# Two token groups of expert 1's second half move into the attention's instruction list, their sums pass through DRAM, and the routing rows get a buffer per group

## The chip, the cores and the metric

The kernel runs on one NeuronCore of one Trainium2 chip. The metric is device time in microseconds (us), less is better. Before the change three runs took 2198.85, 2198.92 and 2199.71 us, median 2198.92. The profile is of one further execution, which took 2201.63 us; its trace spans 2199.9 us. Engines: PE (TensorE), DVE (VectorE), ACT (ScalarE), POOL (GpSimd), and SP (SyncE), whose queue issues most DMAs.

## The reference: what is computed

Three stages follow one another. First a delta-rule attention (4 batches, 8 heads, 768 steps, head size 48), whose output, 3072 tokens by 384, feeds a dense mixture of 8 experts, whose output feeds a second mixture in which each token goes to one expert.

```python
state = state + bt[:, :, :, None] * np.einsum('bhd,bhe->bhde', kt, vt - v_old)     # attention, per step
...
for _ in range(8):                                # first mixture: Sinkhorn-scaled weights P
    P /= P.sum(1, keepdims=True) + 1e-09
    P /= P.sum(0, keepdims=True) + 1e-09
    P *= N / E
for e in range(E):
    out += P[:, e:e + 1] * (np.maximum(x @ w1[e], 0.0) @ w2[e])
...
expert_idx = np.argmax(logits, axis=1)            # second mixture: one expert for each token
out[mask] = gate_w[mask, None] * (np.maximum(x[mask] @ w1[e], 0.0) @ w2[e])
```

Every matrix product is made of three half-precision products (high by high, low by high, high by low), so weights and activations are kept as a high and a low float16 part.

## The kernel before, in words

The tokens lie in 24 tiles of 128 (`NT`), or 6 groups of 512 (`NG`). The hidden size 1024 is 8 blocks of 128 (`KF`); half of it is 4 blocks (`FH`).

**The attention's list.** The attention is written as nodes with costs and dependencies, and `Sched.run` puts them into one order for each engine when the program is built. Into the same list go matmuls of the first mixture: expert 0 whole and the first half of expert 1's hidden blocks, both as units of 256 tokens (`moe_unit`). Their sums need the Sinkhorn weights, which are known only after all of the attention, so they go unscaled to DRAM: ACT copies the sum out of PSUM into the tile `yo` (one buffer), and SP stores it to `y0d` or `y1d`. For these sums the list has one PSUM buffer (`py` in the pool `ps2`). At the list's end stands a piece of expert 1's second half for group 0 of 512 tokens: the first layer (36 matmuls of 512 columns, L1065) and the second layer of the first token tile (12 matmuls of 384 columns, L1078).

**The dense stage.** After the list PE works through the rest of the first mixture in written order. `accb`, the accumulator for 24 tiles, is loaded from `y0d` by six DMAs (L1212). For expert 1 each group loads `yh` from `y1d` (L375); `mlp1` is the first layer, four hidden blocks of nine matmuls, each followed by ACT's relu (high part, L336) and DVE's `hhl` instruction (low part, L337); `mlp2` then makes four token tiles with two PSUM buffers (`py` in `ps3`). Each tile's sum is put into `accb` by ACT's scaling (L384) and two DVE instructions, one for `yh` (L385), one for `py` (L388). Experts 2 to 6 follow with all eight hidden blocks.

**The work beside it.** `run` steps a generator of one group, and after each third step gives one step to every background queue (`bg`). The queue `prepq` holds, in this order: ten empty steps, the preparation of expert 2's weights (`prep_w`: load a half into `st`, six DVE maxima `wmx` at L296, a scale, six ACT and six DVE instructions that split it into `W`; then the other half), `setup2` (a small preparation of the second mixture with a PE transpose `pen`), then the weights of the second mixture. All engines run their instructions in program order. So an instruction that waits holds up what stands behind it on its engine, and this holds for DMAs that SP issues too.

**The routing stage.** Expert 7 and the routing of the second mixture are a second list. For each group `route_group` fills the tile `row` (token number and weight, L1435) and scatters its rows into a DRAM table by four indirect DMAs of POOL (L1461). `row` and the row indices `ri` have two buffers each, so a group takes the buffers of two groups before, and the COPY of L1435 waits until that group's scatter has landed.

Of the kernel before, what the change touches and what calls it, by code (L numbers as in the profile page):

```python
# [165 lines left out]
def kernel(  # L166
# [78 lines left out]
    ones32 = res.tile([128, 128], F32, name="ones32")  # L245
    nc.gpsimd.memset(ones32, 1.0)
    pe = {}
    pye = []
    nc.scalar.activation(out=ivg[0:1], in_=ones32[0:1, 0:1], func=AF.Sqrt)

    def step(gen, n=1):
# [87 lines left out]
    def mlp1(W, XH, XL, n, HH, HL, fs=0):  # L339
        per = 512 // n  # L340
        for f0 in range(fs, KF, per):
            pt = ps1.tile([128, 512], F32, name="pt")
            for j in range(per):
                f = f0 + j
                po = pt[:, j * n:j * n + n]
                i = 0
                for kk in range(KD):
                    for lhsT, rhs in (
                        (w1v(W, 0, kk, f), XH[:, kk, :]),
                        (w1v(W, 0, kk, f), XL[:, kk, :]),  # L350
                        (w1v(W, 1, kk, f), XH[:, kk, :]),
                    ):
                        nc.tensor.matmul(out=po, lhsT=lhsT, rhs=rhs, start=(i == 0), stop=(i == 3 * KD - 1))  # L353
                        i += 1
                    if f == f0 + per - 1 and kk == KD - 1:
                        relu_split(pt, HH[(f0 - fs) // per], HL[(f0 - fs) // per])
                    yield 1

    def mlp2(W, HH, HL, fs=0):
        py = ypool[0].tile([128, 512], F32, name="py")  # L360
        n = 0
        for f in range(fs, KF):
            for lhsT, rhs in ((HH(f - fs), w2v(W, 0, f)), (HH(f - fs), w2v(W, 1, f)), (HL(f - fs), w2v(W, 0, f))):
                nc.tensor.matmul(out=py[:, 0:DM], lhsT=lhsT, rhs=rhs, start=(n == 0), stop=(n == 3 * (KF - fs) - 1))  # L364
                n += 1
            if f < KF - 1:
                yield None
        yield py

    def moe1_group(e, W, g):  # L370

        fs, x = (FH, "b") if e == 1 else (0, e)
        if e == 1:
            yh_ = st2.tile([128, 4, DM], F32, name="yh", tag="yh", bufs=2)
            nc.sync.dma_start(out=yh_, in_=y1d[4 * g:4 * g + 4].rearrange("t p d -> p t d"))  # L375
        if (e, g) != (1, 0):
            yield from mlp1(W, xh[g], xl[g], 512, hh, hl, fs)
        for j in range(4):
            t = 4 * g + j
            sl = slice(128 * j, 128 * j + 128)  # L380
            for py in pye[:1] if (e, t) == (1, 0) else mlp2(W, lambda f: hh[f][:, sl], lambda f: hl[f][:, sl], fs):
                if py is not None:
                    if e == 1:
                        nc.scalar.activation(out=acc[t], in_=acc[t], func=AF.Copy, scale=pe[0][:, t:t + 1])  # L384
                        nc.vector.scalar_tensor_tensor(  # L385
                            out=acc[t], in0=yh_[:, j], scalar=pe[1][:, t:t + 1], in1=acc[t], op0=ALU.mult, op1=ALU.add
                        )
# [31 lines left out]
    with (  # L419
# [446 lines left out]
        def Q(name, eng, cost, fn, deps=(), prio=0.0, **kw):  # L866
            NN[name] = nd(eng, cost, fn, flat(NN[d] for d in deps if d in NN), prio=prio, name=f"{name[0]}.{name[1]}", **kw)
# [111 lines left out]
        def f():  # L979
            nc.sync.dma_start(out=c16, in_=cst16)  # L980
            nc.sync.dma_start(out=cs, in_=cst)
# [75 lines left out]
        o1 = {}
        pn = None
        for f_ in range(FH):
            for kk in range(KD):  # L1060
                def f(slot=None, f_=f_, kk=kk):
                    if kk == 0:
                        o1[f_] = ps1.tile([128, 512], F32, name="pt")
                    for x, (wv, xv) in enumerate(((0, xh), (0, xl), (1, xh))):
                        nc.tensor.matmul(out=o1[f_], lhsT=w1v(W1, wv, kk, FH + f_), rhs=xv[0][:, kk], start=kk == 0 and x == 0, stop=kk == KD - 1 and x == 2)  # L1065
                Q((f"h{f_}_{kk}", "e1"), "P", 648, f, [pn] if pn else [("xb", 0), mend] + w1a, 2e6,
                  ps=("pt", 1) if kk == 0 else None, cols=1536, moe=True)
                pn = (f"h{f_}_{kk}", "e1")
            wr = [mend]
            Q((f"rl{f_}", "e1"), "A", 478, lambda f_=f_: nc.scalar.activation(out=hh[f_], in_=o1[f_], func=AF.Relu), [pn] + wr, NT - 1.0)  # L1070
            Q((f"rs{f_}", "e1"), "V", 602, lambda f_=f_: nc.vector.scalar_tensor_tensor(
                out=hl[f_], in0=o1[f_], scalar=0.0, in1=hh[f_], op0=ALU.max, op1=ALU.subtract), [(f"rl{f_}", "e1")], NT - 1.0, frees=(f"h{f_}_0", "e1"))
        for f_ in range(FH):
            def f(slot=None, f_=f_):
                if f_ == 0:
                    pye.append(ps2.tile([128, 512], F32, name="py"))
                for x, (a_, b_) in enumerate(((hh, 0), (hh, 1), (hl, 0))):
                    nc.tensor.matmul(out=pye[0][:, 0:DM], lhsT=a_[f_][:, 0:128], rhs=w2v(W1, b_, FH + f_),  # L1078
                                     start=(f_ == 0 and x == 0), stop=(f_ == FH - 1 and x == 2))
            Q((f"g{f_}", "e1"), "P", 488, f, [pn, (f"rs{f_}", "e1")] + w1, 2e6, ps=("py", 1) if f_ == 0 else None, cols=1152, moe=True)  # L1080
            pn = (f"g{f_}", "e1")
# [124 lines left out]
    queue(prepq, iter([1] * 10))
    queue(prepq, prep1(2))
    queue(prepq, setup2())
    for e in range(E):
# [3 lines left out]
    for e in range(1, E - 1):  # L1213
        W = Ws[e % 2]
        assert e in wready, e
        if e > 1:
            mk_pe(e)
            prepq.insert(min(1, len(prepq)), prep1(e + 1))
            queue(prepq)
        for g in range(NG):  # L1220
            run(moe1_group(e, W, g))
    while bgs:
        bg()

# [88 lines left out]
    def route_tile(g, j):  # L1313
# [14 lines left out]
        node2(("sn", id_), "A", 520, f, [("acc", t), ("sc", g - 2)], prio=pr)  # L1328

        def f():  # L1330
            o["mx"] = sm.tile([128, 2], F32, name="xmx")
# [54 lines left out]
    def route_group(g):  # L1386
# [19 lines left out]
        lgs = [("lg", 4 * g + j) for j in range(T)]  # L1406
        sns = [("sn", 4 * g + j) for j in range(T)]

        q("m", lambda: vt.tensor_reduce(out=tl("m", [T]), in_=R()[0], op=ALU.max, axis=AX.X), lgs + [("sc", g - 2)], cost=100)
# [6 lines left out]
        q("s1", lambda: vt.tensor_scalar(out=R()[1], in0=R()[1], scalar1=1e-36, scalar2=None, op0=ALU.max), sns + [("sc", g - 2)])  # L1416
# [315 lines left out]
```

## Time and profile before

| what | before |
|---|---|
| runs, us | 2198.85, 2198.92, 2199.71 |
| profiled execution, us | 2201.63 |
| its span, us | 2199.9 |
| PE busy | 2055.6 (93%) |
| DVE busy | 1237.0 (56%) |
| ACT busy | 850.0 (39%) |
| POOL busy | 282.1 (13%) |

Span and busy times are of the profiled execution, with busy time as a share of the span. A row of the trace says when an instruction (or several alike, x12) began, how long it took, and in brackets how long its engine had been idle before it and what ended that. The trace's times count from the span's start; expert 1's dense part runs from 709.7 to 806.1 us, the routing stage from about 1745 to 1985 us.

### The profile page before, as it was taken

The page shows a single profiled execution, that of the slowest core. Times are in us where ns is not written, and L with a number is a line of the kernel's source. Part 1 is how long each engine was busy: PE and PEld are TensorE (multiplying, and loading weights), DVE is VectorE, ACT ScalarE, POOL GpSimd, SP SyncE. Part 2 cuts the span into 40 slices and gives each one's busy share as a digit, 9 for nine tenths or more (in the row PEclk, how much of TensorE's full clock was granted, in tenths as well). Part 3 has the DMA queues.
Part 4 walks back from the last instruction along what each step waited for, and adds up shares of the span by engine and source line. Part 5 has one row for each costly group of instructions (what it writes and reads, how often), then busy time and mean ns, then how long its engine had stood idle before and what let it go on. Part 6 is the DMA issues. An engine that isn't in the chain of part 4 may idle for free. (4 is left out here: it accounts for less than half of the span.)

```text
span 2199.9 us, 46260 instructions
## 1 busy us (share of the span) xinstructions
PE 2055.6 (93%) x19352; PEld 1298.4 (59%) x19352; DVE 1237.0 (56%) x2820; ACT 850.0 (39%) x1594; POOL 282.1 (13%) x324
## 2 busy tenths in 40 slices
PE   3689999989989899999999999999999989999999
PEld 2577777767765445555555555555555545557777
DVE  7988788888763564555545455554553245552111
ACT  6666656566532232232223222322221134352332
POOL 5333223122200000000000000000000000112221
PEclk7589999999999999999999999999999999999999
DMA  4557666566533230222131222213120001049765
GB/s 105 96 105 125 114 110 116 103 117 117 123 110 109 94 105 29 87 84 89 58 115 62 83 87 86 87 58 115 58 87 1 1 19 26 19 126 355 270 237 203
DMA packets 436615, 224.92 MB, mean 102 GB/s; under 512 B 377565, under 2 KB 419329, under 8 KB 430003
## 3 DMA queue, kind: packets, MB, share of 16 engines
q1 hardware_dynamic: 432114, 211.67, 35.9%
q0 software_dynamic: 4288, 10.25, 1.3%
q8 instruction: 154, 2.52, 0.5%
q14 instruction: 59, 0.48, 0.1%
HBM read 138.28 MB, written 50.36 MB: 86 GB/s over the span
## 5 line engine op out<-in xcount | busy, mean ns | idle before, releaser
L353 PE MATMUL pt<-big,W 128*128 128x512 f16 x2340 | 512.8, 379 | 3.5 <-DVE hhl L337 2.0
L353 PEld LDWEIGHTS <-W 128*128 128x128 f16 x2340 | 229.0, 98 | 277.7 <-issue 7.0
L364 PE MATMUL py<-W,hhl 128*128 128x384 f16 x1716 | 302.0, 327 | 8.9 <-DVE accb L388 8.9
L336 ACT ACTIVATE hhl<-pt 128x512 f16<-128x512 f32 x140 | 83.5, 596 | 520.2 <-PE pt L353 514.6
L364 PE MATMUL py<-W,ttb 128*128 128x384 f16 x1440 | 253.6, 326 | 0.0
L364 PEld LDWEIGHTS <-hhl 128*128 128x128 f16 x1716 | 168.4, 98 | 125.3 <-issue 11.6
L388 DVE SCALAR_TENSOR_TENSOR accb<-py,pet,accb 128x384 f32<-128x384 f32 x144 | 88.8, 617 | 197.3 <-PE py L364 195.3
L364 PEld LDWEIGHTS <-ttb 128*128 128x128 f16 x1440 | 140.9, 98 | 93.1
L827 PE MATMUL pt<-xring,W 128*128 128x256 f16 x1296 | 185.0, 277 | 1.4 <-DVE hhl L840 1.0
L337 DVE SCALAR_TENSOR_TENSOR hhl<-pt,hhl 128x512 f16<-128x512 f32 x140 | 96.7, 691 | 149.9 <-ACT hhl L336 149.9
L851 PE MATMUL py<-W,hhl 128*128 128x384 f16 x864 | 174.7, 332 | 5.0 <-ACT yo L861 3.8
L337 DVE SCALAR_TENSOR_TENSOR ttb<-pt,ttb 128x512 f16<-128x512 f32 x120 | 82.9, 690 | 92.7 <-ACT ttb L336 92.6
L296 DVE TENSOR_REDUCE wmx<-st 128x1 f32<-128x512 f32 x168 | 110.4, 677 | 41.1 <-DMA st<-in_moe_w_dram 41.1
L303 POOL PARTITION_ALL_REDUCE wma<-wm x28 | 10.4, 370 | 959.5 <-DVE wm L301 959.5
L336 ACT ACTIVATE ttb<-pt 128x512 f16<-128x512 f32 x120 | 71.5, 596 | 136.9 <-PE pt L353 136.4
L1266 PEld LDWEIGHTS <-W 128*128 128x128 f16 x1008 | 90.6, 98 | 57.1 <-issue 7.1
L827 PEld LDWEIGHTS <-W 128*128 128x128 f16 x1296 | 113.5, 100 | 16.5 <-issue 1.3
L1286 PE MATMUL py<-W,hhl 128*128 128x384 f16 x624 | 110.8, 330 | 0.0
L1266 PE MATMUL pt<-big,W 128*128 128x512 f16 x432 | 98.5, 379 | 5.4 <-DVE hhl L1272 5.4
L851 PEld LDWEIGHTS <-hhl 128*128 128x128 f16 x864 | 74.9, 99 | 44.9 <-issue 7.5
L1272 DVE SCALAR_TENSOR_TENSOR ttb<-pt,ttb 128x512 f16<-128x512 f32 x50 | 34.6, 691 | 113.2 <-ACT ttb L1271 113.1
L1272 DVE SCALAR_TENSOR_TENSOR hhl<-pt,hhl 128x512 f16<-128x512 f32 x52 | 35.8, 688 | 91.2 <-ACT hhl L1271 91.1
(368 smaller groups left out, 3163.3 us busy)
## 6 DMA issues: line engine op xcount, KB each, us to landing
st<-in_moe_w_dram SPq DMA_DIRECT2D x28, 1536.0 KB, 9.9
W<-w2d SPq DMA_DIRECT2D x18, 1536.0 KB, 8.1
w2d<-big SPq DMA_DIRECT2D x16, 1536.0 KB, 6.2
big<-w2d SPq DMA_DIRECT2D x8, 1536.0 KB, 7.7
accb<-w2d SPq DMA_DIRECT2D x8, 1536.0 KB, 9.1
big<-kqc SPq DMA_DIRECT2D x90, 128.0 KB, 3.7
big<-KQ SPq DMA_DIRECT2D x84, 96.0 KB, 3.4
st<-PTc SPq DMA_DIRECT2D x42, 128.0 KB, 3.2
```

Source lines behind the costliest of these rows:

```text
L296: nc.vector.tensor_reduce(out=mx[:, c:c + 1], in_=st[:, c * CW:c * CW + CW], op=ALU.max, axis=AX.X, apply_absolute_value=True)
L303: nc.gpsimd.partition_all_reduce(ma, m1, channels=128, reduce_op=bass.bass_isa.ReduceOp.max)
L336: nc.scalar.activation(out=oh, in_=pt, func=AF.Relu)
L337: nc.vector.scalar_tensor_tensor(out=ol, in0=pt, scalar=0.0, in1=oh, op0=ALU.max, op1=ALU.subtract)
L353: nc.tensor.matmul(out=po, lhsT=lhsT, rhs=rhs, start=(i == 0), stop=(i == 3 * KD - 1))
L364: nc.tensor.matmul(out=py[:, 0:DM], lhsT=lhsT, rhs=rhs, start=(n == 0), stop=(n == 3 * (KF - fs) - 1))
L388: nc.vector.scalar_tensor_tensor(out=acc[t], in0=py[:, 0:DM], scalar=pe[x][:, t:t + 1], in1=acc[t], op0=ALU.mult, op1=ALU.add)
L827: nc.tensor.matmul(out=o[g4][:, 256 * j:256 * j + 256], lhsT=w1v(W, wv, kk, f_), rhs=XR[:, xv, kk], start=(kk == 0 and x == 0), stop=(kk = ...
L851: nc.tensor.matmul(out=o["py"][:, 0:DM], lhsT=a_[f_ // per][:, c_:c_ + 128], rhs=w2v(W, b_, f_), start=(f_ == 0 and x == 0), stop=(f_ == n ...
L1266: nc.tensor.matmul(out=po, lhsT=w1v(W, wv, kk, f), rhs=xv[:, kk, :], start=(kk == 0 and x == 0), stop=(kk == KD - 1 and x == 2))
L1272: V((f"rs{q_}", id_), lambda q_=q_: nc.vector.scalar_tensor_tensor(out=HL[q_], in0=o[q_], scalar=0.0, in1=HH[q_], op0=ALU.max, op1=ALU.sub ...
L1286: nc.tensor.matmul(out=o["py"][:, 0:DM], lhsT=a_[f // per][:, c_:c_ + 128], rhs=w2v(W, b_, f), start=(f == 0 and x == 0), stop=(f == KF - ...
```

## The change

Groups 0 and 1 (`GW = 2`) of expert 1's second half are computed wholly in the attention's list: two first layers and eight second-layer tiles. Their sums are not put into `accb` there; ACT copies each one to `yo` and SP stores it, unscaled, to a new DRAM array `y2d`. In the dense stage expert 1 begins with group 2. The sums of groups 0 and 1 are put into `accb` by a second background queue (`woven_group`), which loads `yg` from `y1d` and `yz` from `y2d` for a tile, scales and adds. The background queues get a step after each second step of expert 1's groups and no longer each third, the ten empty steps are gone, and `yh` is loaded in halves. In the routing `row` and `ri` get one buffer for each group, and the waits on a scatter two groups before become waits on the instructions that last read the other tiles.

```diff
+GW = 2
+    y2d = DR.tile([4 * GW, 128, DM], F32, name="y2d")
...
-        if e == 1:
-            yh_ = st2.tile([128, 4, DM], F32, name="yh", tag="yh", bufs=2)
-            nc.sync.dma_start(out=yh_, in_=y1d[4 * g:4 * g + 4].rearrange("t p d -> p t d"))
+        for j in range(0, 4 if e == 1 else 0, 2):
+            yh_.append(st2.tile([128, 2, DM], F32, name="yh", bufs=2))
+            nc.sync.dma_start(out=yh_[-1], in_=y1d[4 * g + j:4 * g + j + 2].rearrange("t p d -> p t d"))
...
+    def first_acc(t, yh_):
+        nc.scalar.activation(out=acc[t], in_=acc[t], func=AF.Copy, scale=pe[0][:, t:t + 1])
+        nc.vector.scalar_tensor_tensor(out=acc[t], in0=yh_, scalar=pe[1][:, t:t + 1], in1=acc[t], op0=ALU.mult, op1=ALU.add)
+
+    def woven_group(g):
+        for t in range(4 * g, 4 * g + 4):
+            yg = st2.tile([128, DM], F32, name="yg", bufs=2)
+            nc.sync.dma_start(out=yg, in_=y1d[t])
+            yz = st2.tile([128, DM], F32, name="yz", bufs=2)
+            nc.sync.dma_start(out=yz, in_=y2d[t])
+            yield 1
+            yield 1
+            yield 1
+            first_acc(t, yg)
+            nc.vector.scalar_tensor_tensor(
+                out=acc[t], in0=yz, scalar=pe["b"][:, t:t + 1], in1=acc[t], op0=ALU.mult, op1=ALU.add
+            )
+            yield 1
...
+        for g in range(GW):
...
+                def f(t_=t_, g=g, o1=o1):
+                    ob = hp.tile([128, DM], F32, name="yo")
+                    nc.scalar.copy(out=ob, in_=o1["py"][:, 0:DM])
+                    nc.sync.dma_start(out=y2d[4 * g + t_], in_=ob)
+                Q((f"yo{t_}", e1), "A", 413, f, [pn], NT - 1.0, frees=(f"g{t_}_0", e1))
...
-    queue(prepq, iter([1] * 10))
...
-        for g in range(NG):
-            run(moe1_group(e, W, g))
+        if e == 1:
+            queue([], iter([1] * 4), *(woven_group(g) for g in range(GW)))
+        for g in range(GW if e == 1 else 0, NG):
+            run(moe1_group(e, W, g), 2 if e == 1 else 3)
...
-            o["row"] = s2.tile([128, T, 2], I32, name="row")
+            o["row"] = s2.tile([128, T, 2], I32, name="row", bufs=NG)
             vt.tensor_copy(out=o["row"][:, :, 0], in_=toki[:, 4 * g:4 * g + 4])
-        q("ro", f, [("sc", g - 2)])
+        q("ro", f, [])
...
+            o["ri"] = s2.tile([128, T], I32, name="ri", bufs=NG)
```

PE's matmuls keep their order, but for `pen`, which moves to an earlier place. Three other places move. On SP, at the list's end, stood before:

```order
L862 DMA y0d<-yo 128x384 x2
L862 DMA y1d<-yo 128x384 x4
L1212 DMA accb<-y0d 128x4x384 x6
L375 DMA yh<-y1d 128x4x384 x2
L287 DMA st<-in_moe_w_dram 128x3x1024
L375 DMA yh<-y1d 128x4x384 x2
```

and there stands now:

```order
L879 DMA y1d<-yo 128x384 x4
L1107 DMA y2d<-yo 128x384 x8
L1238 DMA accb<-y0d 128x4x384 x6
L377 DMA yh<-y1d 128x2x384 x2
L288 DMA st<-in_moe_w_dram 128x3x1024
L398 DMA yg<-y1d 128x384
L400 DMA yz<-y2d 128x384
```

The eight stores to `y2d`, each behind an ACT copy of a list tile, have come ahead of the loads of `accb`, and the weight load into `st` still follows behind `yh`.

On DVE, from the list's end on, stood before:

```order
L1071 SCALAR_TENSOR_TENSOR hhl<-pt,hhl 128x512 x4
L385 SCALAR_TENSOR_TENSOR accb<-yh,pet,accb 128x384
L388 SCALAR_TENSOR_TENSOR accb<-py,pet,accb 128x384
L385 SCALAR_TENSOR_TENSOR accb<-yh,pet,accb 128x384
L388 SCALAR_TENSOR_TENSOR accb<-py,pet,accb 128x384
L385 SCALAR_TENSOR_TENSOR accb<-yh,pet,accb 128x384
L388 SCALAR_TENSOR_TENSOR accb<-py,pet,accb 128x384
L385 SCALAR_TENSOR_TENSOR accb<-yh,pet,accb 128x384
L388 SCALAR_TENSOR_TENSOR accb<-py,pet,accb 128x384
L337 SCALAR_TENSOR_TENSOR hhl<-pt,hhl 128x512 x4
```

and there stands now:

```order
L1091 SCALAR_TENSOR_TENSOR hhl<-pt,hhl 128x512 x8
L338 SCALAR_TENSOR_TENSOR hhl<-pt,hhl 128x512 x3
L297 TENSOR_REDUCE wmx<-st 128x1
L338 SCALAR_TENSOR_TENSOR hhl<-pt,hhl 128x512
L297 TENSOR_REDUCE wmx<-st 128x1 x2
L393 SCALAR_TENSOR_TENSOR accb<-yh,pet,accb 128x384
L386 SCALAR_TENSOR_TENSOR accb<-py,pet,accb 128x384
L297 TENSOR_REDUCE wmx<-st 128x1
L393 SCALAR_TENSOR_TENSOR accb<-yg,pet,accb 128x384
L405 SCALAR_TENSOR_TENSOR accb<-yz,pet,accb 128x384
L297 TENSOR_REDUCE wmx<-st 128x1
```

The first maximum over `st` now stands ahead of the fourth `hhl` of the first dense group, where before the dense stage began with additions into `accb`.

On DVE, in the routing stage, while PE is in a group's second layer, stood before:

```order
L1456 CAST qri<-qrr 128x4
L1272 SCALAR_TENSOR_TENSOR ttb<-pt,ttb 128x512 x3
L1435 COPY row<-toki 128x4
L1272 SCALAR_TENSOR_TENSOR ttb<-pt,ttb 128x512
L1477 SCALAR_TENSOR_TENSOR accb<-py,pet,accb 128x384
```

and there stands now:

```order
L1486 CAST ri<-qrr 128x4
L1300 SCALAR_TENSOR_TENSOR ttb<-pt,ttb 128x512 x4
L1508 SCALAR_TENSOR_TENSOR accb<-py,pet,accb 128x384
L1360 TENSOR_REDUCE xmx<-accb 128x1
L1362 TENSOR_SCALAR xmx<-xmx 128x1
```

The COPY into `row` no longer stands among the `ttb` instructions; all six copies stand at the head of the routing stage.

## Rows read from the trace of the kernel before

**Rows 1.** Timeline of PE: start us, duration us, line, operation; in brackets idle, releaser.

```profile
698.05 2.11 PE L851 MATMUL py<-W,hhl 128*128 128x384 f16 x12 [0.61 <-ACT yo L861]
700.00 7.93 PE L1065 MATMUL pt<-big,W 128*128 128x512 f16 x36
707.77 2.11 PE L1078 MATMUL py<-W,hhl 128*128 128x384 f16 x12
709.72 4.06 PE L364 MATMUL py<-W,hhl 128*128 128x384 f16 x24
722.34 4.00 PE L364 MATMUL py<-W,hhl 128*128 128x384 f16 x12 [8.56 <-DVE accb L388]
...
742.02 7.93 PE L353 MATMUL pt<-big,W 128*128 128x512 f16 x36
...
806.08 9.88 PE L353 MATMUL pt<-big,W 128*128 128x512 f16 x45
817.14 0.35 PE L1157 MATMUL pen<-cs,ench 8*128 8x8 f32 x3 [1.19 <-DVE ench L1152]
```

**Rows 2.** Windows: busy us (and count) of PE, PEld, DVE, ACT, POOL; clock, DMA, GB/s.

```profile
715.00:720.00 5.00, 0.00 (x0) 0.00 (x0) 0.31 (x1) 0.00 (x0) 0.00 (x0) 0.65 1.06 373
720.00:722.30 2.30, 0.00 (x0) 0.00 (x0) 2.08 (x5) 0.00 (x0) 0.00 (x0) 0.50 1.06 414
...
709.70:806.10 96.40, 86.92 (x459) 45.30 (x457) 57.01 (x104) 30.23 (x54) 1.68 (x4) 0.95 0.36 123
806.10:839.20 33.10, 31.67 (x173) 16.72 (x172) 15.13 (x39) 7.82 (x13) 0.35 (x1) 1.00 0.08 30
```

**Rows 3.** Timeline of DVE, routing stage.

```profile
1806.59 0.17 DVE L1435 COPY row<-toki 128x4 int32<-128x4 int32 x1 [9.77 <-DMA tab<-row,qri]
```

**Rows 4.** Timeline of PE, routing stage.

```profile
1799.20 1.95 PE L1286 MATMUL py<-W,ttb 128*128 128x384 f16 x11
1807.41 0.50 PE L1286 MATMUL py<-W,ttb 128*128 128x384 f16 x1 [6.26 <-DVE ttb L1272]
...
1811.55 1.95 PE L1286 MATMUL py<-W,ttb 128*128 128x384 f16 x9
```

**Rows 5.** Timeline of PE, next group's boundary.

```profile
1847.31 0.34 PE L1286 MATMUL py<-W,ttb 128*128 128x384 f16 x1 [1.77 <-DVE ttb L1272]
```

**Rows 6.** Timeline of ACT: the last two copies of the list.

```profile
697.52 0.48 ACT L861 COPY yo<-py 128x384 f32<-128x384 f32 x1 [1.69 <-PE py L851]
700.24 0.48 ACT L861 COPY yo<-py 128x384 f32<-128x384 f32 x1 [2.24 <-PE py L851]
```

**Rows 7.** The list's stores of yo (whole span to 720): from issue to landing, us.

```profile
DMA to landing us min/median/max: 1.8/1.8/4.4
```

**Rows 8.** Timeline of the DMAs that SP issues.

```profile
701.25 5.47 SPq L1212 DMA_DIRECT2D accb<-y0d  x6
706.77 4.96 SPq L375 DMA_DIRECT2D yh<-y1d  x2
```

**Rows 9.** The page's DMA issues: KB of one, median us to landing.

```profile
st<-in_moe_w_dram SPq DMA_DIRECT2D x28, 1536.0 KB, 9.9
```

**Rows 10.** Timeline of DVE, dense stage of expert 1 and after.

```profile
719.69 0.62 DVE L385 SCALAR_TENSOR_TENSOR accb<-yh,pet,accb 128x384 f32<-128x384 f32 x1 [10.40 <-DMA yh<-y1d]
...
752.41 0.61 DVE L385 SCALAR_TENSOR_TENSOR accb<-yh,pet,accb 128x384 f32<-128x384 f32 x1
753.14 0.62 DVE L388 SCALAR_TENSOR_TENSOR accb<-py,pet,accb 128x384 f32<-128x384 f32 x1
753.67 0.68 DVE L296 TENSOR_REDUCE wmx<-st 128x1 f32<-128x512 f32 x1
...
762.59 0.75 DVE L276 SCALAR_TENSOR_TENSOR W<-st,w0s,W 128x512 f16<-128x512 f32 x1 [0.73 <-ACT W L275]
...
815.77 0.15 DVE L1109 RECIPROCAL nrc<-nsr 8x1 f32<-8x1 f32 x1 [2.29 <-ACT nsr L1107]
```

**Rows 11.** The second half's load into st, 760 to 800 us.

```profile
DMA to landing us min/median/max: 7.0/7.0/7.0
```

More of the change, by code (lines that the diff above doesn't have):

```diff
@@ L247 @@
     pe = {}
-    pye = []
     nc.scalar.activation(out=ivg[0:1], in_=ones32[0:1, 0:1], func=AF.Sqrt)
@@ L372, in moe1_group @@
         fs, x = (FH, "b") if e == 1 else (0, e)
-        if e == 1:
-            yh_ = st2.tile([128, 4, DM], F32, name="yh", tag="yh", bufs=2)
-            nc.sync.dma_start(out=yh_, in_=y1d[4 * g:4 * g + 4].rearrange("t p d -> p t d"))
-        if (e, g) != (1, 0):
-            yield from mlp1(W, xh[g], xl[g], 512, hh, hl, fs)
+        yh_ = []
+        for j in range(0, 4 if e == 1 else 0, 2):
+            yh_.append(st2.tile([128, 2, DM], F32, name="yh", bufs=2))
+            nc.sync.dma_start(out=yh_[-1], in_=y1d[4 * g + j:4 * g + j + 2].rearrange("t p d -> p t d"))
+        yield from mlp1(W, xh[g], xl[g], 512, hh, hl, fs)
         for j in range(4):
@@ L380, in moe1_group @@
             sl = slice(128 * j, 128 * j + 128)
-            for py in pye[:1] if (e, t) == (1, 0) else mlp2(W, lambda f: hh[f][:, sl], lambda f: hl[f][:, sl], fs):
+            for py in mlp2(W, lambda f: hh[f][:, sl], lambda f: hl[f][:, sl], fs):
                 if py is not None:
                     if e == 1:
[L384 to L387, printed above, removed]
+                        first_acc(t, yh_[j // 2][:, j % 2])
                     nc.vector.scalar_tensor_tensor(
@@ L1055 @@
             Q(("xb", g), "D", 1300, f, bigdeps(g) + [("x1", 4 * g + 1), ("x1", 4 * g + 3)], NT + 1.0 + g, lat=1500.0)
[L1057 to L1081, printed above, removed]
+        pn = mend
@@ new lines, with f @@
+        for g in range(GW):
+            e1 = f"e1{g}"
+            o1 = {}
+            wr = pn
+            for f_ in range(FH):
+                for kk in range(KD):
+                    def f(slot=None, f_=f_, kk=kk, g=g, o1=o1):
+                        if kk == 0:
+                            o1[f_] = ps1.tile([128, 512], F32, name="pt")
+                        for x, (wv, xv) in enumerate(((0, xh), (0, xl), (1, xh))):
+                            nc.tensor.matmul(out=o1[f_], lhsT=w1v(W1, wv, kk, FH + f_), rhs=xv[g][:, kk], start=kk == 0 and x == 0, stop=kk == KD - 1 and x == 2)
+                    Q((f"h{f_}_{kk}", e1), "P", 648, f, [pn] if f_ or kk else [pn, ("xb", g)] + w1a, 2e6 + g,
+                      ps=("pt", 1) if kk == 0 else None, cols=1536, moe=True)
+                    pn = (f"h{f_}_{kk}", e1)
+                Q((f"rl{f_}", e1), "A", 478, lambda f_=f_, o1=o1: nc.scalar.activation(out=hh[f_], in_=o1[f_], func=AF.Relu), [pn, wr], NT - 1.0)
+                Q((f"rs{f_}", e1), "V", 602, lambda f_=f_, o1=o1: nc.vector.scalar_tensor_tensor(
+                    out=hl[f_], in0=o1[f_], scalar=0.0, in1=hh[f_], op0=ALU.max, op1=ALU.subtract), [(f"rl{f_}", e1)], NT - 1.0, frees=(f"h{f_}_0", e1))
+            for t_ in range(4):
+                for f_ in range(FH):
+                    def f(slot=None, f_=f_, t_=t_, o1=o1):
+                        if f_ == 0:
+                            o1["py"] = ps2.tile([128, 512], F32, name="py")
+                        for x, (a_, b_) in enumerate(((hh, 0), (hh, 1), (hl, 0))):
+                            nc.tensor.matmul(out=o1["py"][:, 0:DM], lhsT=a_[f_][:, 128 * t_:128 * t_ + 128], rhs=w2v(W1, b_, FH + f_),
+                                             start=(f_ == 0 and x == 0), stop=(f_ == FH - 1 and x == 2))
+                    Q((f"g{t_}_{f_}", e1), "P", 488, f, [pn, (f"rs{f_}", e1)] + w1, 2e6 + g, ps=("py", 1) if f_ == 0 else None, cols=1152, moe=True)
+                    pn = (f"g{t_}_{f_}", e1)
+                def f(t_=t_, g=g, o1=o1):
[3 more added lines that the diff above has]
+                Q((f"yo{t_}", e1), "A", 413, f, [pn], NT - 1.0, frees=(f"g{t_}_0", e1))
@@ L1327, in f @@
             nc.scalar.activation(out=junk, in_=acc[t], func=AF.Square, accum_out=R()[1][:, j:j + 1])
-        node2(("sn", id_), "A", 520, f, [("acc", t), ("sc", g - 2)], prio=pr)
+        node2(("sn", id_), "A", 520, f, [("acc", t), ("rw", g - 2)], prio=pr)
         def f():
@@ L1407, in route_group @@
         sns = [("sn", 4 * g + j) for j in range(T)]
-        q("m", lambda: vt.tensor_reduce(out=tl("m", [T]), in_=R()[0], op=ALU.max, axis=AX.X), lgs + [("sc", g - 2)], cost=100)
+        q("m", lambda: vt.tensor_reduce(out=tl("m", [T]), in_=R()[0], op=ALU.max, axis=AX.X), lgs + [("ri", g - 2), ("rw", g - 2)], cost=100)
         q("l2", lambda: vt.tensor_tensor(out=tl("l2", [T, E]), in0=R()[0], in1=b3(o["m"]), op=ALU.subtract), ["m"], cost=100)
@@ L1414, in route_group @@
         q("oh", lambda: vt.tensor_tensor(out=tl("oh", [T, E], F16), in0=b2_(eio), in1=b3(o["fi"]), op=ALU.is_equal), ["fi"], cost=100)
-        q("s1", lambda: vt.tensor_scalar(out=R()[1], in0=R()[1], scalar1=1e-36, scalar2=None, op0=ALU.max), sns + [("sc", g - 2)])
+        q("s1", lambda: vt.tensor_scalar(out=R()[1], in0=R()[1], scalar1=1e-36, scalar2=None, op0=ALU.max), sns + [("rw", g - 2)])
         q("s0", lambda: nc.scalar.activation(out=tl("sr", [T]), in_=R()[1], func=AF.Ln), ["s1"], "A", 220)
@@ L1455, in route_group, with f @@
         q("rr", lambda: vt.tensor_reduce(out=tl("rr", [T]), in_=o["rk"], op=ALU.add, axis=AX.X), ["rm"], cost=100)
-        q("ri", lambda: vt.tensor_copy(out=tl("ri", [T], I32), in_=o["rr"]), ["rr"])
+        def f():
+            o["ri"] = s2.tile([128, T], I32, name="ri", bufs=NG)
+            vt.tensor_copy(out=o["ri"], in_=o["rr"])
+        q("ri", f, ["rr"])
         def f():
```

## The prediction, made before the changed kernel had run

> **What bounds the kernel now.** I read the busy times of the engines first: PE is busy in 93% of the span, so a change moves the time where it opens or closes a gap of PE, or lets another engine pass it. Then I read PE's timeline, bracket by bracket, in the two stretches that the change touches. At the list's end PE runs the list's last first layer and one tile (700.00 to 709.72), then two tiles of the dense stage, and then it waits 8.56 us for DVE [rows 1]. DVE's timeline names what DVE waited for: `yh`, which landed at about 719.5 [rows 10], behind the six loads of `accb` on the same queue [rows 8]. PE comes back at the lower of its two clocks, 1.2 GHz (granted share 0.50 in the window before it resumes [rows 2]): 12 matmuls take 4.00 us for 2.11 [rows 1]. In the routing stage PE waits 6.26 us and then 1.77 us for a `ttb` instruction of DVE [rows 4, 5]; DVE stood at the COPY into `row`, 9.77 us the first time, until a scatter had landed [rows 3]. Last I read the windows for how full DVE is in expert 1's dense part: 57.0 us in 96.4 [rows 2].
>
> All sums are made against the profiled execution, 2201.63 us, which is 2.7 above the median 2198.92; I put the differences on the median. PE's order is unchanged but for `pen`, so I follow PE from 700.00.
>
> **Step 1, the list gets longer.** From start to start a first layer takes 7.77 us (700.00 to 707.77) and a tile 1.95 us (707.77 to 709.72) where the next may follow at once [rows 1]. In the list there is one PSUM buffer, and each tile waits for ACT's copy of the one before: the copies of such a pair lie 2.72 us apart [rows 6], with PE idle 0.61 [rows 1]. So a group costs 7.77 + 1.95 + 3 x 2.72 = 17.9 us, two 35.8, and the dense stage begins at 735.8. `yo` has one buffer too, so a copy needs the store before it to have landed: 0.48 + 1.8 = 2.3 us, under 2.72 [rows 6, 7]; with the longest landing, 4.4, the six pairs would cost 2.2 us more each, 13 in all, my upper bound. Before, group 2 began at 742.02 [rows 1], so PE is 6.2 us ahead here: the old wait and its slow clock are gone, 3 x 2 x 0.77 = 4.6 us is paid for copies.
>
> The Trainium skill, "DMA: Bandwidth & Descriptors", section "Anatomy of one DMA — SWDGE (gpsimd) path", puts a DMA at 2.0 us plus its bytes at 436 GB/s, most of the 2.0 being the receipt of the write. By this a store of 192 KB takes 2.45 us, a copy cannot follow before 2.9 us, and step 1 would cost about 1.3 us more; the row with 1.8 decides.
>
> **Step 2, the loads start late.** SP issues in order, and the first load of `accb` stands right behind the last store: it was issued at 701.25, 1.25 us after the matmuls that follow the last stored tile began [rows 8, 1]. That was 8.5 us ahead of the dense stage. Now eight more stores stand ahead of it, the last behind a copy at the list's very end, so the first load goes out at 735.8 + 1.25 = 737.0, when dense work has already begun. Before, DVE had the first `yh` 18.4 us after that issue (719.69 less 701.25): seven transfers of 768 KB. Now these are followed by expert 2's weights, 1536 KB [rows 9], 4.2 us more at the 373 GB/s of the full queue [rows 2]. So `st` is there at 737.0 + 18.4 + 4.2 = 759.7.
>
> **Step 3, a new wait.** The ten empty steps were what kept DVE's first maximum over `st` away from this load. Now it stands ahead of the fourth `hhl` of group 2, which PE needs for the last quarter of its first tile. PE ends the first layer at 743.5 and three quarters of a tile at 745.0. DVE resumes at 759.7, runs one maximum (0.6) and the `hhl` (0.7), and PE goes on at 761.0: 16.0 us idle in place of 8.56. The slow clock afterwards costs the 1.9 us of [rows 1]. Left of expert 1 are then 0.5 + 3 x 1.95 + 3 x 15.57 = 53.1 us (a dense group is 7.77 + 4 x 1.95), so without any further wait it ends at 816.0, against 806.08 before [rows 1]: 9.9 us later.
>
> **Step 4, DVE becomes the bound.** The additions of groups 0 and 1 are still made in the dense stage, so DVE keeps its 48 additions, while PE loses two groups to the list. DVE's work before was 57.0 us; four `hhl` fewer make 54.2. To this come `setup2` and the first maxima of the next preparation, as the steps now run faster: they were 15.1 us of the next window less eight `hhl`/`ttb` (5.5) and four additions (2.5), about 7 [rows 2]. Three `hhl` come before the stall (2.1), which leaves about 59 us behind 759.7. An addition that depends on the one before starts 0.73 us after it, though one lasts 0.61 [rows 10]; over the 24 pairs that is some 2 us more: 61. And DVE waits in it, for reasons that its order fixes: the second half of the weights can be loaded only when the first has been split, lands 7.0 us after its issue [rows 11], and DVE has about 4 us of additions and `hhl` to do meanwhile (3); twice the first split waits for ACT (0.73 each [rows 10], 1.5); the root in `setup2` takes ACT 2.3 us, behind ACT's queue (3) [rows 10]; `pen` sends DVE to PE and back, with the `hhl` behind it (3); four short ones for PE (2). That is 12.5, so DVE's last addition of expert 1 ends near 759.7 + 61 + 12.5 = 833, and PE, at most two tiles ahead of it, leaves expert 1 at about 832. Late against before: 832 - 806.1 = 26. I see this on PE as waits for `hhl` in the second and third dense group (2 to 3 us each), one for `py` of about 3 us while the second weight half lands, and one of 3 to 4 at `pen`. In the next expert `pen`'s 1.2 us is saved [rows 1]: 24.8. The bounds are 9.9 (DVE hides all) and 32 (those 3 us waits also lower the clock).
>
> **Step 5, the routing rows.** Both COPYs that waited for a scatter now stand at the stage's head and wait for nothing. PE's tiles, 3.9 us each here, would have been at 1799.20 + 2 x 1.95 = 1803.1 where the row says 1811.55: 8.45 us [rows 4]. The second wait is 1.77 [rows 5]. What is late next? The last `ttb` could have followed its predecessor by 1.9 us and be done 2 us before PE's need, and no other instruction of DVE or ACT waits for a scatter. Gain 10.2; from the other side at least 0, if PE stopped for something hidden behind.
>
> The extra traffic (1.5 MB stored and loaded again) is hidden: the queue has 0.36 of its time taken in this stretch [rows 2]. The eight loads from `y1d` replace two of equal bytes.
>
> **Sum.** +26 - 1.2 - 10.2 = +14.6, so 2198.92 + 14.6 = 2213.5; rounded, 2213.
>
> **Rivals.**
> - *DVE keeps pace.* Steps 2 and 3 hold, but DVE fits its work into PE's 55 us. Then +9.9 - 1.2 - 10.2 = -1.5: 2197.4, no change that can be measured. For it: DVE's busy share before was 59% [rows 2]. Against: 59 us do not go into 55. Values between, down to 2206, belong to the forecast. Chance 0.14.
> - *The loads go out early.* If SP could issue the loads of `accb`, `yh` and `st` ahead of the last stores, there would be no stall; expert 1 would end at 735.8 + 62.3 = 798 plus some 5 us of DVE, and the time would be -3 - 1.2 - 10.2 = -14: about 2185. It decides if the loads go out more than about 16 us before 737.0. For it: before, they went out while the list still ran. Against: SP's rows show the loads right behind the store [rows 8], and eight stores stand ahead. Chance 0.12.
> - *Worse.* DVE's waits make gaps of 3 us or more on PE with the slow clock behind them, or a new wait takes the place of the routing one: +32 - 11.4 = +20.6, or +26 - 1.2 = +24.8. About 2222. Chance 0.12.
> - *Faster transfers.* If the burst moved at 414 GB/s, as one window shows, and not 373 [rows 2], 7.1 MB would land 2 us sooner: 2211, inside the forecast. By the fit of the Trainium skill named above the same burst would take 2.0 + 16.2 = 18.2 us and not 22.6, and the time would be 2209; the trace's 373 GB/s speaks against this. Chance 0.03, counted as slower.
>
> **How the numbers follow.** The forecast has 0.59, with its own range 2205 to 2219. One measurement of this kernel tells no difference under about 0.2%, 4.4 us. Faster by more: 0.12 (early loads), and 0.01 of the second. Within: 0.13 of "DVE keeps pace" and 0.02 of the forecast's low end, 0.15. Slower: 0.72. The range, 2197 to 2221, leaves out the early loads and about half of "worse".
>
> **What would show it.** Step 1: PE's first dense matmul of expert 1 at about 736, six gaps of 0.6 before it. Step 2: the first load of `accb` at about 737, behind the last store. Step 3: one gap of PE of 14 to 18 us in the first dense tile, released by `hhl`, while DVE waits for `st`. Step 4: expert 1 ends at about 832, with several waits of PE for DVE. Step 5: no wait of PE for `ttb` in the routing stage, which is 10 us shorter. The prediction is wrong if the large gap is missing or DVE stays ahead of PE after it.

## The result, and the profile after

Five runs of the changed kernel took 2209.23 to 2221.81 us, median 2213.31; five of the kernel before took 2198.85 to 2202.32, median 2199.71. The ratio is 1.0055, with an interval of 1.0041 to 1.0069: the change makes the kernel slower by 12 us by the ratio, 13.6 by the medians. The forecast was 2213. Here the sum can be held against the trace, and its terms do not all agree.

| what | before | after |
|---|---|---|
| median of five runs, us | 2199.71 | 2213.31 |
| profiled execution, us | 2201.63 | 2214.02 |
| its span, us | 2199.9 | 2212.2 |
| expert 1's second half, from the list's first layer on | 106.08 (700.00 to 806.08) | 130.45 (699.68 to 830.13) |

PE's timeline after, in the place of [rows 1] (start us, duration us, line, operation; in brackets idle, releaser):

```profile
699.68 7.93 PE L1086 MATMUL pt<-big,W 128*128 128x512 f16 x36
...
710.17 2.11 PE L1099 MATMUL py<-W,hhl 128*128 128x384 f16 x12 [0.61 <-ACT yo L1106]
...
735.45 7.93 PE L354 MATMUL pt<-big,W 128*128 128x512 f16 x36
743.22 1.95 PE L365 MATMUL py<-W,hhl 128*128 128x384 f16 x11
759.42 8.77 PE L365 MATMUL py<-W,hhl 128*128 128x384 f16 x37 [14.25 <-DVE hhl L338]
768.02 4.05 PE L354 MATMUL pt<-big,W 128*128 128x512 f16 x18
774.05 5.73 PE L354 MATMUL pt<-big,W 128*128 128x512 f16 x18 [1.98 <-DVE hhl L338]
...
787.00 2.11 PE L365 MATMUL py<-W,hhl 128*128 128x384 f16 x12 [1.21 <-DVE accb L386]
...
795.49 5.68 PE L354 MATMUL pt<-big,W 128*128 128x512 f16 x18 [2.50 <-DVE hhl L338]
...
815.12 0.35 PE L1184 MATMUL pen<-cs,ench 8*128 8x8 f32 x3 [2.04 <-DVE ench L1179]
815.40 7.04 PE L354 MATMUL pt<-big,W 128*128 128x512 f16 x24
822.27 8.01 PE L365 MATMUL py<-W,hhl 128*128 128x384 f16 x48
830.13 11.82 PE L354 MATMUL pt<-big,W 128*128 128x512 f16 x54
```

There are six gaps of 0.61 in the list, one of 14.25 in the first dense tile, then waits of 1.98, 1.21, 2.50, 0.15, 1.05 and 2.04 us, all for DVE. The three that are near 2 us or above are each followed by matmuls that take longer: 18 of 512 columns run in 5.73 us where others take 4.05.

What SP issued there, in the place of [rows 8]:

```profile
710.15 26.37 SPq L1107 DMA_DIRECT2D y2d<-yo  x8
736.69 5.32 SPq L1238 DMA_DIRECT2D accb<-y0d  x6
742.06 3.10 SPq L377 DMA_DIRECT2D yh<-y1d  x2
745.26 1.27 SPq L288 DMA_DIRECT2D st<-in_moe_w_dram  x1
```

For 26 us SP does nothing but store list tiles, and the first load of `accb` goes out at 736.69. DVE's timeline shows who pays, in the place of [rows 10]:

```profile
742.10 0.69 DVE L338 SCALAR_TENSOR_TENSOR hhl<-pt,hhl 128x512 f16<-128x512 f32 x1 [1.25 <-ACT hhl L337]
758.08 0.69 DVE L297 TENSOR_REDUCE wmx<-st 128x1 f32<-128x512 f32 x1 [15.28 <-DMA st<-in_moe_w_dram]
758.68 0.68 DVE L338 SCALAR_TENSOR_TENSOR hhl<-pt,hhl 128x512 f16<-128x512 f32 x1
...
785.01 0.69 DVE L297 TENSOR_REDUCE wmx<-st 128x1 f32<-128x512 f32 x1 [1.38 <-DMA st<-in_moe_w_dram]
```

The `hhl` that PE needs needs nothing from that load; it stands behind the maximum. The windows, in the place of [rows 2] (busy us and count of PE, PEld, DVE, ACT, POOL; granted clock, DMA share, GB/s):

```profile
735.40:830.10 94.70, 71.53 (x341) 34.93 (x339) 58.88 (x122) 32.65 (x58) 1.76 (x5) 0.86 0.52 179
752.00:759.40 7.40, 0.00 (x0) 0.00 (x0) 1.32 (x3) 0.00 (x0) 0.00 (x0) 0.50 1.00 377
776.00:777.90 1.90, 1.90 (x6) 0.63 (x5) 1.76 (x3) 0.60 (x1) 0.00 (x0) 0.50 0.00 0
```

The queue is full (377 GB/s) while PE stands, and the third row shows a granted clock of 0.50, PE's lower level of 1.2 GHz, behind a wait of 1.98 us.

In the routing stage the waits of PE (us in total, times, longest), of the kernel before:

```profile
PE py L1286 <- DVE ttb L1272: 8.0, 2, 6.3
PE px L1597 <- DMA xg<-x2d,tb: 1.4, 1, 1.4
```

and after:

```profile
PE pt L1294 <- DVE hhl L1300: 5.4, 5, 1.1
PE px L1628 <- DMA xg<-x2d,tb: 2.6, 1, 2.6
```

The two waits for `ttb` [rows 4, 5] are gone; the five for `hhl` stood there before too, also 5.4 in sum. Where the difference arises is read from boundaries on PE: the end of expert 1 (806.08 and 830.13, above), expert 2's second group and the routing stage. The last two before:

```profile
839.16 9.88 PE L353 MATMUL pt<-big,W 128*128 128x512 f16 x45
...
1746.10 15.70 PE L1266 MATMUL pt<-big,W 128*128 128x512 f16 x72
```

and after:

```profile
861.73 11.82 PE L354 MATMUL pt<-big,W 128*128 128x512 f16 x54
...
1767.40 15.70 PE L1294 MATMUL pt<-big,W 128*128 128x512 f16 x72
```

The kernel is 24.05 us late when expert 1 ends, 22.57 when expert 2's second group begins, 21.3 when the routing stage begins, and 12.3 at the end: the routing stage and what follows are 9.0 us shorter.

### The profile page after: what moved, and what is told of

Read it like the earlier page. It is cut to its first block, busy times and chain, and to the rows that moved or that the text cites. A ratio compares the mean times of both kernels' runs of the same rounds, so it can differ in the third digit from the quotient of the medians.

```text
span 2212.2 us, 46321 instructions
## 1 busy us (share of the span) xinstructions
PE 2058.7 (93%) x19352; PEld 1298.8 (59%) x19352; DVE 1237.2 (56%) x2820; ACT 853.8 (39%) x1602; POOL 282.4 (13%) x324
## 4 chain that ended last, share of the span: by engine, by line
PE 70%; DVE 12%; DMA 8%; ACT 5%; issue 3%; SPq 2%; POOL 0%; DVEq 0%; ACTq 0%; POOLq 0%
PE py L365 21%; PE pt L354 21%; PE py L1314 8%; PE pt L1294 7%; PE py L868 4%; PE pt L844 3%; DMA st<-in_moe_w_dram 1%; DVE Z L497 1%; DMA big<-kqc 1%; DVE tt L685 1%; SPq L562 1%; PE py L1099 1%; PE pz L478 1%; PE pt L1086 1%; SPq L489 1%
## 5 line engine op out<-in xcount | busy, mean ns | idle before, releaser
L365 PE MATMUL py<-W,hhl 128*128 128x384 f16 x1632 | 288.9, 328 | 16.7 <-DVE hhl L338 14.2
L365 PEld LDWEIGHTS <-hhl 128*128 128x128 f16 x1632 | 160.4, 98 | 128.6 <-DVE hhl L338 14.9
L386 DVE SCALAR_TENSOR_TENSOR accb<-py,pet,accb 128x384 f32<-128x384 f32 x136 | 83.8, 617 | 196.9 <-PE py L365 195.3
L868 PE MATMUL py<-W,hhl 128*128 128x384 f16 x864 | 175.7, 334 | 4.4 <-ACT yo L878 3.4
L304 POOL PARTITION_ALL_REDUCE wma<-wm x28 | 10.2, 362 | 960.4 <-DVE wm L302 960.4
L1314 PE MATMUL py<-W,hhl 128*128 128x384 f16 x624 | 109.0, 326 | 0.0
L868 PEld LDWEIGHTS <-hhl 128*128 128x128 f16 x864 | 75.5, 100 | 44.9 <-issue 8.7
```

The source lines that it names most:

```text
L386: nc.vector.scalar_tensor_tensor(out=acc[t], in0=py[:, 0:DM], scalar=pe[x][:, t:t + 1], in1=acc[t], op0=ALU.mult, op1=ALU.add)
L868: nc.tensor.matmul(out=o["py"][:, 0:DM], lhsT=a_[f_ // per][:, c_:c_ + 128], rhs=w2v(W, b_, f_), start=(f_ == 0 and x == 0), stop=(f_ == n ...
L1314: nc.tensor.matmul(out=o["py"][:, 0:DM], lhsT=a_[f // per][:, c_:c_ + 128], rhs=w2v(W, b_, f), start=(f == 0 and x == 0), stop=(f == KF - ...
```

## The experiments

All were timed beside the kernel before, whose medians on these chips were 2203.08 (first four) and 2202.31 (last four). In the traces the list's last first layers begin at different times, 693.1 to 702.6 us, even between kernels whose instructions up to there are the same; so stages are compared by their length from there.

**1. The routing rows alone**, added to the kernel before, with the changed waits that belong to them:

```diff
...
-            o["row"] = s2.tile([128, T, 2], I32, name="row")
+            o["row"] = s2.tile([128, T, 2], I32, name="row", bufs=NG)
...
-        q("ro", f, [("sc", g - 2)])
+        q("ro", f, [])
...
+            o["ri"] = s2.tile([128, T], I32, name="ri", bufs=NG)
```

> The kernel before with the routing rows' part of the change alone (row and ri with one buffer for each group, no wait on a scatter). Theory: both waits of PE for ttb in the routing stage go, 8.45 + 1.77 us, and nothing else moves: 2199.7 - 10.2 = about 2189.5, ratio 0.9953. Rival, another wait takes their place or the gain belongs to the list's part: 2199.7, ratio 1.000, with a new gap of PE in the routing stage.

2193.94 us, ratio 0.9957 (0.9943 to 0.9971): 9.5 us gained by the ratio, 10.2 expected. In its trace no wait for `ttb` is left in the routing stage, and no new one of that size has come.

**2. The list's part alone**, the changed kernel with its routing rows as before:

```diff
...
-            o["row"] = s2.tile([128, T, 2], I32, name="row", bufs=NG)
+            o["row"] = s2.tile([128, T, 2], I32, name="row")
...
-        q("ro", f, [])
+        q("ro", f, [("sc", g - 2)])
...
```

> The changed kernel with the routing rows as they were before. Theory: the two parts add, so the list's part alone costs 13.6 + 10.2 = 23.8: about 2223.5, ratio 1.011, with PE's waits for ttb of 6.3 and 1.8 us back in the routing stage and the same 14 us gap in the first dense tile. Rival, the parts hide each other (a later start of the routing stage shifts the scatters): 2213, ratio 1.006.

2224.19 us, ratio 1.0106 (1.0080 to 1.0132): 23 us lost. Its trace has two waits for `ttb` in the routing stage again (8.4 us in sum) and the gap in the first dense tile (14.57). The two parts add, -0.43% and +1.06%, to +0.63%, within the interval of the whole. So the change is a gain and a larger loss, and the question is what the loss is made of: the late loads, or DVE.

**3. The stores on ACT's queue**, so that SP can issue the loads while the list still runs:

```diff
-                    nc.sync.dma_start(out=y2d[4 * g + t_], in_=ob)
+                    nc.scalar.dma_start(out=y2d[4 * g + t_], in_=ob)
```

> The changed kernel with the eight stores to y2d issued from ACT's queue, right behind the copy, so that SP's loads of accb have no store ahead of them that waits for the list. Theory: the first load of accb goes out at about 701 and no longer at 736.7, the gap of 14.25 us in the first dense tile and the slow clock behind it (2.6) go: 2213.3 - 17 = about 2196, ratio 0.9985, while PE's later waits for DVE in the dense stage (8.9 us in sum) stay, since DVE's work there is as much as before. Rival 1, these later waits are only the backlog of the gap: they go too, about 2188, ratio 0.995. Rival 2, the loads are bound by something else than the stores (buffers, the queue): they go out late as before, 2213, ratio 1.006.

2211.0 us, ratio 1.0031 (1.0021 to 1.0041): about 5 us better than the changed kernel by the ratios, but a miss by 10 us against the expected ratio. The loads did go out early (first `accb` load at 703.06) and the gap of 14 us is gone. But the stores now meet the burst of loads. ACT's timeline:

```profile
711.78 0.48 ACT L1106 COPY yo<-py 128x384 f32<-128x384 f32 x1 [1.40 <-PE py L1099]
712.29 0.34 ACTq L1107 DMA_DIRECT2D y2d<-yo  x1
717.82 0.48 ACT L1106 COPY yo<-py 128x384 f32<-128x384 f32 x1 [5.55 <-DMA y2d<-yo]
718.32 0.33 ACTq L1107 DMA_DIRECT2D y2d<-yo  x1
724.52 0.48 ACT L1106 COPY yo<-py 128x384 f32<-128x384 f32 x1 [6.23 <-DMA y2d<-yo]
```

and PE's:

```profile
712.31 2.11 PE L1099 MATMUL py<-W,hhl 128*128 128x384 f16 x12 [0.61 <-ACT yo L1106]
718.35 3.79 PE L1099 MATMUL py<-W,hhl 128*128 128x384 f16 x12 [3.92 <-ACT yo L1106]
725.05 3.72 PE L1099 MATMUL py<-W,hhl 128*128 128x384 f16 x12 [2.92 <-ACT yo L1106]
...
746.49 7.93 PE L354 MATMUL pt<-big,W 128*128 128x512 f16 x36
```

A store of 192 KB keeps the one buffer `yo` for 5.5 to 6.2 us, where alone it lands in 1.8 [rows 7]; twice PE waits (3.92 and 2.92 us) and then runs at its slow clock. The list takes 44.67 us (701.82 to 746.49) for 35.77. The Trainium skill, "DMA: Bandwidth & Descriptors", section "Issuing engines are not separate DMA queues", says that DMAs of all issuing engines run on the same 16 DMA engines and interleave. The trace agrees that another issuing engine does not free a store from the loads. The dense part still took 78.93 us (746.49 to 825.42), with waits for DVE of 11.2 us in sum: early loads alone do not make DVE keep pace.

**4. DVE's added work moved one expert on**, on top of 3: the additions of groups 0 and 1 run beside expert 2, which takes its groups in the order 2, 3, 4, 5, 0, 1.

```diff
-        if e == 1:
+        if e == 2:
             queue([], iter([1] * 4), *(woven_group(g) for g in range(GW)))
-        for g in range(GW if e == 1 else 0, NG):
+        for g in [*range(GW, NG), *range(0 if e > 1 else GW, GW)] if e < 3 else range(NG):
```

> store_act, and the additions of groups 0 and 1 (woven_group, 16 DVE and 8 ACT instructions) moved from expert 1's to expert 2's stage, which then takes the groups in the order 2, 3, 4, 5, 0, 1. Theory, DVE is the bound of expert 1's dense stage: with some 10 us less of DVE work there, PE's waits for DVE fall from about 9 us to under 3, and the time is 6 us under store_act's: about 2190, ratio 0.9955. Rival, the waits come from the order of single instructions (loads into st, the root in setup2) and not from the load: as store_act, 2196, ratio 0.9985.

2204.35 us, ratio 1.0012 (0.9997 to 1.0026): about 4 us under 3. It has 3's waits in the list, in this trace longer still (48.8 us for 44.7; why is open). The dense part, however, shrank from 78.9 to 69.8 us, and PE's waits for DVE in it fell from 11.2 to 5.9, not to under 3 as expected.

**5. The ten empty steps put back** into the changed kernel, so that the first maximum no longer stands ahead of the first dense group's `hhl`:

```diff
+    queue(prepq, iter([1] * 10))
     queue(prepq, prep1(2))
```

> The changed kernel with the ten empty steps put back ahead of expert 2's weight preparation. Theory: the first maximum over st no longer stands ahead of the fourth hhl; the first gap of PE in the dense stage moves to the third tile's py, waits for yh (landed at about 754) and shrinks from 14.3 to 8 or 9 us. But DVE stays the bound of the stage: what it does not do early it does later, so expert 1 ends within 3 us of where it ended: 2213, between 2209 and 2214, ratio 1.0035 to 1.006. Rival, the gap alone makes the loss: 5.5 us and the slow clock less, 2207 or under, ratio 1.003 or under.

2214.0 us, ratio 1.0066 (1.0041 to 1.0091), four runs between 2205.9 and 2220.8: no gain that can be told. PE's timeline:

```profile
694.29 7.93 PE L1086 MATMUL pt<-big,W 128*128 128x512 f16 x36
...
730.09 7.93 PE L354 MATMUL pt<-big,W 128*128 128x512 f16 x36
737.86 4.06 PE L365 MATMUL py<-W,hhl 128*128 128x384 f16 x24
749.13 5.82 PE L365 MATMUL py<-W,hhl 128*128 128x384 f16 x24 [7.20 <-DVE accb L386]
...
1761.02 15.70 PE L1295 MATMUL pt<-big,W 128*128 128x512 f16 x72
```

The gap shrinks from 14.25 to 7.20 us and is now a wait for the additions, which wait for `yh`; later waits for DVE are a little longer (11 us in sum). So in the trace the maximum's place makes about half of the gap and the late loads the other half. The dense part is 7 us shorter than the changed kernel's, where the expectation allowed 3. But it does not last: from expert 2's second group to the routing stage PE waits 6.6 us for DVE, for 2.0 in the changed kernel, and from the list's first layer to the routing stage the two take 1066.7 and 1067.7 us. So what DVE does not do early it does later, as expected, only not all of it within expert 1. The traced execution, 2205.9, is the lowest of the four because its list came to its last part 5.4 us earlier.

**6. Stores on ACT's queue with five staging buffers**, 3 with one edit more, so that no copy waits for a store:

```diff
-                    ob = hp.tile([128, DM], F32, name="yo")
+                    x_ = 768 * ((4 * g + t_) % 5)
+                    ob = ttb[:, x_:x_ + 768].bitcast(F32)
```

> store_act with five buffers for the list's stored sums (in the tile ttb, free at that time) in place of one. Theory: in store_act the stores queued behind the early loads and the one buffer made PE wait 6.8 us, with slow clock behind; with five no copy waits for a store, the dense stage begins 9 us earlier than in store_act (some 35.8 us after the list's last part began) and the time falls by 9: ratio 1.0031 - 0.0041 = 0.999. Rival: the ACT queue's own DMA issues wait for earlier transfers, so the relus behind them come late and the gain is under 3 us, ratio 1.002 or more.

2198.54 us, ratio 0.9979 (0.9967 to 0.9990), 0.999 expected. The list is back at 35.5 us, the gap of 14 us is gone too, and yet the dense part takes 80.0 us, with waits for DVE of 10.9 us in sum. Its window:

```profile
735.40:815.40 80.00, 69.10 (x341) 34.19 (x340) 59.01 (x122) 32.53 (x58) 1.75 (x5) 0.94 0.34 114
```

**7. Both, 6 and 4:**

> yo5 with the additions of groups 0 and 1 in expert 2's stage, as in woven_late. Theory, the two effects add: 9 us of the list and 9 us of DVE's bound under store_act: ratio 1.0031 - 0.0082 = about 0.995, some 10 us faster than before. Rival: with the list's wait gone DVE's waits come back, no more than half of it: 0.999.

2193.12 us, ratio 0.9961 (0.9947 to 0.9975), 0.995 expected. The window of the dense part:

```profile
728.60:798.40 69.80, 63.95 (x342) 32.79 (x340) 49.83 (x106) 28.30 (x50) 1.75 (x5) 1.00 0.32 108
```

16 additions fewer take 9.2 us of work from DVE (59.01 to 49.83), and the stage is 10.2 us shorter: 5.1 in waits (10.9 to 5.8) and the rest in the clock (0.94 to 1.00). So the additions set the pace there; the run takes away 16 DVE instructions together with their eight ACT scalings and their loads, and does not part these. DVE is not busy all the time even in 6 (59.01 of 80.00 us): the order in which it waits counts too, and `pen`'s wait of 2.03 us stays in 7 as it was. Of the 10.2 us, 4.4 come back as two waits for `hhl` beside expert 2 (2.02 and 2.38), where the additions now run. From the list's first layer to the routing stage this kernel takes 1046.2 us and the kernel before 1046.1: with both mends the list's part costs nothing and gains nothing, and the ratio is that of the routing rows alone.

**8. The kernel before with one load moved**, and the routing rows of 1: the first group's `yh` is loaded right behind the first load of `accb`, ahead of the other five; nothing goes into the list.

```diff
         nc.sync.dma_start(out=accb[:, 4 * g:4 * g + 4], in_=y0d[4 * g:4 * g + 4].rearrange("t p d -> p t d"))
+        if g == 0:
+            yh0.append(load_yh(0))
...
-            yh_ = st2.tile([128, 4, DM], F32, name="yh", tag="yh", bufs=2)
-            nc.sync.dma_start(out=yh_, in_=y1d[4 * g:4 * g + 4].rearrange("t p d -> p t d"))
+            yh_ = yh0[0] if g == 0 else load_yh(g)
```

> Not the list's part at all: the kernel before, with the routing rows' part, and the first group's yh loaded right behind the first accb load and no longer behind all six. Theory: PE's wait of 8.56 us was one for the order of these loads; with yh 0 landing at about 709 it goes, and the slow clock behind it (1.9) too: with the rows 10.4 + 10 us under before, ratio 0.9905. Rival: the next load on the queue is late in its place (accb 1 or yh 1) and PE waits at group 1: 0.9945 or more.

2178.61 us, ratio 0.9892 (0.9875 to 0.9908): the best of all, faster than both kernels. What SP issued:

```profile
700.52 1.11 SPq L1218 DMA_DIRECT2D accb<-y0d  x1
701.69 0.50 SPq L374 DMA_DIRECT2D yh<-y1d  x1
702.24 6.87 SPq L1218 DMA_DIRECT2D accb<-y0d  x5
```

and PE's timeline:

```profile
709.00 6.01 PE L364 MATMUL py<-W,hhl 128*128 128x384 f16 x36
714.85 7.93 PE L353 MATMUL pt<-big,W 128*128 128x512 f16 x36
...
794.49 9.88 PE L353 MATMUL pt<-big,W 128*128 128x512 f16 x45
```

The wait of 8.56 us and the slow clock behind it [rows 1] are gone; from the list's first layer expert 1 takes 95.2 us (699.28 to 794.49), where before took 106.08 and the changed kernel 130.45. The first addition depended on two of the seven transfers only. Against experiment 1 the moved load is worth 14 us by the ratios (0.9957 to 0.9892) and 10.9 by expert 1's length, 10.4 expected; the intervals of the ratios allow both.

## Why the prediction was right, and which terms were off

The net came out right, and the mechanism is the one forecast. Pure PE work from the list's first layer to the end of expert 1 is 6 x 7.77 + 24 x 1.95 = 93.4 us [rows 1]; what is above that, in the profiled execution:

| term, us | predicted | measured |
|---|---|---|
| step 1, copies in the list | 4.6 | 4.6 (35.77 less 31.14) |
| step 3, the gap | 16.0 | 14.25 |
| step 3, slow clock behind it | 1.9 | 2.6 |
| step 4, waits for DVE | 16.0 (832 less 816.0) | 8.9 |
| step 4, slow clock behind these | 0 | 5.0 |
| the rest: ends of matmuls ahead of each gap, `pen` | 0 | 1.7 |
| sum | 38.5 | 37.05 (130.45 less 93.4) |

**Step 1** was right: 35.77 us for two groups, six gaps of 0.61. The stores landed 1.9 us after issue and never decided there; the 2.45 us of the prediction are by a fit of the Trainium skill whose section is on DMAs that GpSimd issues, and SP issues these. The landing did decide in experiment 3, when they met the loads.

**Step 2** was right in place (736.69, predicted 737.0), and its end came 1.6 us earlier than predicted: DVE had `st` at 758.08, 21.4 us after the first load was issued and not 22.6. The burst ran at 374 and 377 GB/s (745 to 752 and 752 to 759.4 us), 373 in the rows of before; experiments 3 and 6, where the loads go out early and the gap goes, show that without this place on SP's queue there is no gap, although the maximum stands ahead of the `hhl` there too.

**Step 3** was right in mechanism: one gap in the first dense tile, released by an `hhl` behind a maximum that waited for `st`. Mis-sized were the gap (14.25 for 16.0, by step 2's 1.6) and the clock (37 matmuls took 8.60 us from start to start, where 37 x 0.1625 is 6.0).

**Step 4**, DVE the bound: experiments 6 and 7 bear it out, where the additions of groups 0 and 1 are the difference. The end of expert 1 was predicted at 832 and came at 830.13; DVE's last addition of its groups ended at 831.9, predicted 833. But the makeup of PE's loss was wrong: the step that was mis-sized. I counted all of PE's loss as idle time and put the slow clock behind such waits into the rival "Worse". It came: three waits of 1.98, 2.50 and 2.04 us were each followed by matmuls at a granted clock of 0.50 for part of their length, 1.7 us each time (18 matmuls from 774.05 to 779.62 took 5.57 for 3.89). The waits themselves were 8.9 us and not 16. So a part of that rival was true at the total that I had forecast; its time of 2222 did not come.

That the total held all the same is not chance in the main. From `st` to its last addition DVE took 73.8 us (758.08 to 831.91), predicted 73.5, and PE, at most two tiles ahead, loses what DVE needs, as idle time or as slow clock. Experiment 2's trace bears this out: there a wait of 2.59 us had no slow clock behind it, but the waits that followed were longer, and from the end of the large gap to the third dense group PE took 29.24 us, 29.53 in the changed kernel. Luck was in DVE's own idle time, 12.7 us for 12.5: the second weight half and the root cost 1.4 and 1.8 for 3 each, but the `hhl` behind `pen`, where DVE waits for ACT behind a PE at its slow clock, 4.6 for 3, and the short waits 3.5 for 2.

**`pen`** saved 1.48 us in expert 2's first group (24.05 less 22.57), predicted 1.2.

**Step 5** was right: 10.2 predicted, 9.0 in the trace, 9.5 in experiment 1. In the trace the missing 1.2 is the wait for the first gathered rows `xg`, 2.6 us for 1.4.

**The rivals.** "DVE keeps pace" fell: even with the loads early, DVE's waits stayed (experiments 3 and 6). "Loads early" was wrong for this kernel, and its price was wrong too: it allowed 5 us for DVE behind a list without the gap, and experiment 6, which makes just that case, lost 17.7 in the dense part (80.0 less 62.3), and came out 4.6 us under the kernel before by its ratio, where 14 was put. "Faster transfers" fell with 374 to 377 GB/s.

**Where the intended gain went.** PE's work is the same; two groups only changed places. The list gave them no idle time to fill and took 4.6 us for copies; the loads behind the wait of 8.56 us, which the longer list could have covered, were pushed behind that list on their own queue; and DVE kept all 48 additions for four groups of PE work in place of nearly six. The maximum's place makes about 7 of the gap's 14 us (experiment 5's trace), but moving it back alone gains nothing by the routing stage.

## What to carry to other kernels

Before work is moved to cover a wait, look at what the wait's own transfer stands behind: here moving one load ahead of five others won 14 us by the ratios (10.9 in the trace), where moving two groups of matmuls lost 23. A store that waits for a computation holds up every load behind it on its queue, so what a stage needs first must be issued ahead of it. And when work of the bounding engine moves out of a stage, count what its helpers still have to do there: the next engine may become the bound.

## What was not expected of the hardware

- Waits of about 2 us cost clock as well: after 1.98, 2.50 and 2.04 us of idle PE ran for part of the next matmuls at a granted clock of 0.50. Not every such wait did: in the kernel of experiment 2 a wait of 2.59 us was followed by nine matmuls at a granted clock of 1.00 (timeline, then window), and behind `pen`'s wait of 2.03 there 24 matmuls took 5.35 us, for 7.04 behind 2.04 in the changed kernel. What decides between the two is open.

```profile
775.14 2.10 PE L354 MATMUL pt<-big,W 128*128 128x512 f16 x9 [2.59 <-DVE hhl L338]
...
775.10:777.30 2.20, 2.10 (x9) 0.87 (x9) 2.17 (x4) 1.07 (x2) 0.00 (x0) 1.00 0.47 167
```

- A store of 192 KB issued by ACT held its buffer for 5.5 to 6.2 us while SP's loads filled the queue, against 1.9 us without them.
